# Mish in a fused attention, expert and MLP kernel: a square on ScalarE, the low half on VectorE

## The chip, the core and the metric

One core of one Trainium2 chip runs the whole program. Times are device microseconds (us) of one execution. TensorE (PE) does the matmuls, VectorE (DVE), ScalarE (ACT) and GpSimd (POOL) the elementwise work; each engine runs its own instructions strictly in the order in which the program issued them, and engines meet only at semaphores.

## What is computed

Causal attention over 4 batches of 8 heads and 576 positions, then a mixture of 8 experts with a capacity of 288 tokens each, and then, for every token, a second MLP with one set of weights. The part that the change touches is the activation of the second MLP:

```python
def _moe2_ref(x, w_in, w_out):          # x: 2304 x 512, w_in: 512 x 2048, w_out: 2048 x 512
    h = x @ w_in
    sp = np.where(h > 20.0, h, np.log1p(np.exp(np.minimum(h, 20.0))))
    g = h * np.tanh(sp)
    return (g @ w_out).astype(np.float32)
```

With a = e^h, tanh(log(1 + a)) is (a² + 2a) / (a² + 2a + 2), so that g can be had from Exp and Ln alone. `w_in` and `w_out` arrive as 64-bit floats.

## The kernel before, in words

Attention runs first, up to about 330 us; the routing of expert 0 follows. Then eight experts run one after the other, from 391 us on, and each has two stages. The up stage, `up(e)`, is the expert's own two matrices with Relu between them. The down stage, `down(e)`, takes the expert's 288 tokens through the second MLP. Both the experts and the second MLP work with split operands: every float32 matrix is a high half (rounded by ACT) and a low half (the rest), and each product is three matmuls, high by high, high by low, low by high (`mm3`, L444 to L446).

A down stage has 16 steps f, one for each 128 of the 2048 hidden rows. A step makes one PSUM tile `hp` by 12 matmuls (4 chunks by 3), hands it to `mish(f, p, gs)`, and then multiplies the finished activation of step f − 3 (`LAG = 3`) into four output tiles `y`, 12 matmuls again. In the first three steps there is no activation yet and only the first half is done; the last three have only the second half. `ps_h` has three `hp` banks.

The order on the engines is written out by hand. `tick()` is called in the middle and at the end of each half step, so there are four ticks in a full step. A tick runs what `later(n, ...)` had put n ticks ahead, then one step of `conv`, then perhaps one step of the routing of the next expert, `route(e + 1)`, whose VectorE operations (masks L248, one-hot blocks `ohs` L355, and many small ones) and small matmuls (`rt`, L253 to L360) so stand between those of the second MLP.

`mish` as it was: L531 takes min(h, 20) out of PSUM (DVE), L532 is Exp (ACT). Two ticks later `part1`: L535 b = (a + 2)·a on DVE, L536 Ln(b + 2) and L537 Exp(−) on ACT, L538 t = b·h on DVE, which is the last reader of the `hp` bank. Four ticks after the start `part2`: L542 t·a on DVE, L543 the high half by ACT (a Copy that rounds), L544 the low half by POOL. In the last two steps the delays are one and two ticks. `a`, `b` and `t` are three tiles of a ring `c1` of six.

Other work on the same engines: `split` of the expert weights (L413 ACT, L414 POOL), and in the first down stage still the conversion of the second MLP's weights from 64-bit words. A unit of that takes three DVE operations, L101, L104 and L107, on a tile of the same ring `c1`, one operation a tick, and then L83 on ACT and L84 on POOL.

Of the kernel before, what the change touches and what calls it, by code (L numbers as in the profile page):

```python
# [8 lines left out]
F32 = mybir.dt.float32  # L9
F32R = mybir.dt.float32r  # L10
# [4 lines left out]
AF = mybir.ActivationFunctionType  # L15
OP = mybir.AluOpType
# [7 lines left out]
CAP = N // E  # L24
# [3 lines left out]
def fb(ap):  # L28
    return ap.bitcast(F32)


class Convert:
    """The second MLP's weights: raw words to float32, split into hi and lo, in resident tiles."""

    def __init__(self, nc, w_in, w_out, ring):
        self.nc, self.w_in, self.w_out, self.ring = nc, w_in, w_out, ring
# [5 lines left out]
        self.steps = self.run()  # L42

    def slots(self):
        """Places for float32 words ahead of the split, in tiles that the experts need only later."""
        NC = DM // 128
        for name, n, words in (("xu", 1, 2 * NC * CAP), ("act", 4, 2 * CAP), ("ot", 1, NC * CAP)):
            for _ in range(n):
                t = self.ring(name, [128, words], I32)
                for j in range(words // 256):  # L50
                    yield t[:, 256 * j:256 * j + 256].rearrange("p (c f) -> p c f", c=2)
# [64 lines left out]


def constants(nc, one, K):
    """The expert choice's constants, one instruction or two a step."""

    def new(name, shape, dt):
        K[name] = one.tile(shape, dt, name=name)
        return K[name]

    def iota(name, shape, dt, pattern, base, mult):
        nc.gpsimd.iota(new(name, shape, dt), pattern=pattern, base=base, channel_multiplier=mult,
                       allow_small_or_imprecise_dtypes=True)

    iota("jj", [128, 63], F32, [[1, 63]], 1, 0)
    yield  # L130
    nc.gpsimd.memset(new("onesb", [128, 128], BF16), 1.0)
    yield
    upper = new("upper", [128, 128], BF16)
    nc.gpsimd.memset(upper, 1.0)
    yield
    nc.gpsimd.affine_select(out=upper, in_=upper, pattern=[[1, 128]], compare_op=OP.is_gt, fill=0.0,
                            base=0, channel_multiplier=-1)
    yield
    iota("slots", [128, CAP // 3], FP16, [[1, CAP // 3]], 0, 0)
    yield  # L140
    aux = new("aux", [128, NT, 3, 2], BF16)[:, :, 0]
    nc.gpsimd.iota(aux[:, 0:16, 0].rearrange("p (b i) -> p b i", b=B), pattern=[[S, B], [128, 4]], base=0,
                   channel_multiplier=0, allow_small_or_imprecise_dtypes=True)
    yield
    for r in range(2):
        nc.gpsimd.iota(aux[64 * r:64 * r + 64, 16:18, 0], pattern=[[2 * S, 2]], base=512 + 512 * r,
                       channel_multiplier=0, allow_small_or_imprecise_dtypes=True)
        yield
    nc.gpsimd.iota(aux[:, :, 1], pattern=[[0, NT]], base=0, channel_multiplier=1,
                   allow_small_or_imprecise_dtypes=True)  # L150
    yield
    iota("erow", [128, E], F32, [[-1, E]], E, 0)
    yield
    jj, th1, j20 = K["jj"], new("th1", [128, 63], I32), new("j20", [128, 63], F32)
    x1 = j20.bitcast(I32)
    nc.vector.tensor_scalar(th1, jj, -32.0, float(2 ** 26), op0=OP.add, op1=OP.mult)
    yield
    nc.vector.tensor_scalar(x1, th1, 31, 0x7FFFFFFF, op0=OP.arith_shift_right, op1=OP.bitwise_and)
    yield
    nc.vector.tensor_tensor(th1, th1, x1, op=OP.bitwise_xor)  # L160
    yield
    nc.vector.tensor_scalar(j20, jj, float(2 ** 20), None, op0=OP.mult)
    yield
    K["steps"] = []
    at = 20
    for i, nb in enumerate((5, 5, 5, 5)):
        at -= nb
        r = new(f"jr{i}", [128, 2 ** nb - 1], F32)
        nc.vector.tensor_scalar(r, jj[:, :2 ** nb - 1], float(2 ** at), None, op0=OP.mult)
        K["steps"].append((2 ** nb - 1, float(2 ** at), r))  # L170
        yield
    nc.vector.memset(new("cb", [128, 2 * NT], F32)[:, 0:1], 4096.0)


def build(ctx, tc, q, k, v, s, w_gate, w1, w2, w_in, w_out, out, debug=None):
# [22 lines left out]
    with ExitStack() as actx:  # L198
        attention(actx, tc, const, cv, q, k, v, s, w_gate, ident, L, x_dram, b_dram, constants(nc, const, K))
# [9 lines left out]
def experts(ctx, tc, K, ring, ident, L, x_dram, w1, w2, cv, out):  # L209
    nc = tc.nc  # L210
    NF1, NF2, NC, NJ, JW = F // 128, F2 // 128, DM // 128, 3, CAP // 3
    rot = ctx.enter_context(tc.tile_pool(name="m_rot", bufs=2))
    one = ctx.enter_context(tc.tile_pool(name="m_one", bufs=1))
# [8 lines left out]
    WI, WO = cv.WI, cv.WO  # L222

    jj, onesb, upper, slots, aux, erow, th1, j20, cb = (K[n] for n in (
        "jj", "onesb", "upper", "slots", "aux", "erow", "th1", "j20", "cb"))
    steps = K["steps"]
# [163 lines left out]
    raw, wt = {}, {}  # L390
# [61 lines left out]
    def later(n, fn, *args):  # L452
        todo.setdefault(now[0] + n, []).append((fn, args))
# [71 lines left out]
    spacer = one.tile([1, 1], F32, name="spacer")  # L525

    def mish(f, p, gs):
        a = rot.tile([128, CAP], F32, name="c1", bufs=6)
        b = rot.tile([128, CAP], F32, name="c1", bufs=6)
        t = rot.tile([128, CAP], F32, name="c1", bufs=6)  # L530
        nc.vector.tensor_scalar(a, p[:, :CAP], 20.0, None, op0=OP.min)  # L531
        nc.scalar.activation(a, a, AF.Exp)  # L532

        def part1():
            nc.vector.scalar_tensor_tensor(b, a, 2.0, a, op0=OP.add, op1=OP.mult)  # L535
            nc.scalar.activation(a, b, AF.Ln, bias=2.0)  # L536
            nc.scalar.activation(a, a, AF.Exp, scale=-1.0)  # L537
            nc.vector.tensor_mul(t, b, p[:, :CAP])  # L538

        def part2():  # L540
            g = ring("act", [128, 2, CAP], F32R)
            nc.vector.tensor_mul(t, t, a)  # L542
            nc.scalar.activation(g[:, 0], t, AF.Copy)  # L543
            nc.gpsimd.tensor_sub(g[:, 1], t, fb(g)[:, 0])  # L544
            gs[f] = g
        tail = f >= NF2 - 2
        later(1 if tail else 2, part1)
        later(2 if tail else 4, part2)

    def down(e):  # L550
        x2 = X2.pop(e)
# [3 lines left out]
        for f in range(NF2 + LAG):  # L555
            if f < NF2:
                need(f, 0)
                p = ps_h.tile([128, 512], F32, name="hp")
                for c in range(NC):
                    mm3(p[:, :CAP], (WI[f][:, 0, c], WI[f][:, 1, c]), (x2[:, 0, c], x2[:, 1, c]),  # L560
                        c == 0, c == NC - 1)
                    if c == 1:
                        tick()
                mish(f, p, gs)
                if f > 1:
                    feed(0 if f < NF2 - 6 else 1)
                tick()
            if f == NF2 and e + 1 < E:
                while side["route"] is not None:
                    tick()  # L570
                feed()
            if f >= NF2 and e + 1 < E:
                make_xt(e + 1, [f - NF2])
            if f >= LAG:
                need(f - LAG, 1)
                g = gs.pop(f - LAG)
                w = WO[f - LAG]
                for c in range(NC):
                    cs = slice(128 * c, 128 * c + 128)
                    mm3(o[c][:, :CAP], (w[:, 0, cs], w[:, 1, cs]), hl(g), f == LAG, f == NF2 + LAG - 1)  # L580
                    if c == 1:
                        tick()
                tick()
# [540 lines left out]
```

## Time and profile before

| | us |
|---|---|
| median of 3 runs | 1151.33 (1151.16 to 1170.0) |
| span of the profiled execution | 1157.2 |
| busy in that span: PE, DVE, ACT, POOL | 1018.5, 820.7, 569.4, 556.7 |

The profile is of one execution, and its span runs from the first to the last instruction; here it is 5.9 us over the median of the runs shown, so that a sum made in the span is carried to the median as a difference. The profile lists, for each engine and line, how long its instructions took and what ended the idle time before them, and it can be cut to a stretch of the span. An instruction's time is from its start to its end; where it had to wait for something after it had started, that is in its time and not in the idle time.

### The profile page before, as it was taken

The numbers are of one execution on the slowest core, as the hardware profiler recorded it, in microseconds if no ns is written. First come the engines' busy times: TensorE is split into PE (matmuls) and PEld (weight loads), VectorE is DVE, ScalarE is ACT, GpSimd is POOL, SyncE is SP. The second block draws the span as 40 slices with busy tenths as digits, with TensorE's granted clock in tenths as the row PEclk, the third lists the DMA queues.
The fourth block names the chain that finished last, engine by engine and source line by source line (L and its number), as shares of the span: only waits on it lengthen the run. The fifth ranks groups of instructions, "written<-read, shape, count | busy, mean of one in ns | idle before, by whom it ended". The sixth has DMA issues, their size and how long they took to land. (4 is left out here: it accounts for less than half of the span.)

```text
span 1157.2 us, 21785 instructions
## 1 busy us (share of the span) xinstructions
PE 1018.5 (88%) x7739; PEld 955.5 (83%) x7739; DVE 820.7 (71%) x2137; ACT 569.4 (49%) x1269; POOL 556.7 (48%) x567
## 2 busy tenths in 40 slices
PE   6889899889941778799999999999999999999996
PEld 5778788778830778788998988998899898899996
DVE  7566577777579889976876876776677577687274
ACT  5466557555751335443553553454454355355453
POOL 6355556455556653554256256256235324625622
PEclk8798889887875789999999999999999899999998
DMA  5687898887132532322123123023012112312300
GB/s 113 135 167 157 183 185 181 172 183 174 50 94 93 166 117 64 120 62 71 38 58 94 38 58 94 1 87 96 6 56 86 48 38 62 90 38 57 95 1 21
DMA packets 133657, 105.60 MB, mean 91 GB/s; under 512 B 63052, under 2 KB 113388, under 8 KB 133516
## 3 DMA queue, kind: packets, MB, share of 16 engines
q1 hardware_dynamic: 121596, 83.49, 30.2%
q10 hardware_dynamic: 8880, 11.27, 3.1%
q0 software_dynamic: 3072, 9.44, 2.7%
q8 instruction: 61, 1.00, 0.4%
q14 instruction: 48, 0.39, 0.1%
HBM read 69.55 MB, written 9.73 MB: 69 GB/s over the span
## 5 line engine op out<-in xcount | busy, mean ns | idle before, releaser
L544 POOL TENSOR_TENSOR act<-c,act 128x288 fp32r<-128x288 f32 x128 | 105.6, 826 | 295.8 <-ACT act L543 283.4
L945 POOL TENSOR_TENSOR Pl<-P,Ph 128x384 fp32r<-128x384 f32 (+2 forms) x128 | 136.1, 1068 | 135.1 <-DVE Ph L944 47.4
L414 POOL TENSOR_TENSOR wt<-raw,wt 128x512 fp32r<-128x512 f32 x128 | 169.0, 1335 | 64.5 <-ACT wt L413 62.6
L444 PE MATMUL y<-act,WO 128*128 128x288 f32 x512 | 157.3, 307 | 0.4
L445 PE MATMUL y<-act,WO 128*128 128x288 f32 x512 | 153.1, 299 | 3.7 <-POOL act L544 3.2
L444 PE MATMUL hp<-xu,WI 128*128 128x288 f32 x512 | 154.7, 302 | 0.0
L446 PE MATMUL y<-act,WO 128*128 128x288 f32 x512 | 152.1, 297 | 0.0
L445 PE MATMUL hp<-xu,WI 128*128 128x288 f32 x512 | 152.1, 297 | 0.0
L446 PE MATMUL hp<-xu,WI 128*128 128x288 f32 x512 | 151.6, 296 | 0.0
L535 DVE SCALAR_TENSOR_TENSOR c<-c 128x288 f32<-128x288 f32 x128 | 88.8, 694 | 49.7 <-ACT c L532 49.7
L543 ACT ACTIVATE act<-c 128x288 fp32r<-128x288 f32 x128 | 56.9, 445 | 112.5 <-DVE c L542 107.6
L413 ACT ACTIVATE wt<-raw 128x512 fp32r<-128x512 f32 x128 | 79.6, 624 | 56.0 <-PE y L446 29.1
L445 PEld LDWEIGHTS y<-act,WO 128*128 128x128 f32 x512 | 97.3, 190 | 6.2 <-POOL act L544 5.5
L444 PEld LDWEIGHTS y<-act,WO 128*128 128x128 f32 x512 | 97.3, 190 | 5.8 <-ACT c L532 2.1
L446 PEld LDWEIGHTS y<-act,WO 128*128 128x128 f32 x512 | 97.5, 190 | 0.0
L444 PEld LDWEIGHTS hp<-xu,WI 128*128 128x128 f32 x512 | 97.2, 190 | 0.3
L445 PEld LDWEIGHTS hp<-xu,WI 128*128 128x128 f32 x512 | 97.2, 190 | 0.0
L446 PEld LDWEIGHTS hp<-xu,WI 128*128 128x128 f32 x512 | 97.1, 190 | 0.0
L937 ACT ACTIVATE P<-s 128x384 f32<-128x384 f32 (+2 forms) x128 | 64.1, 503 | 62.5 <-PE s L930 42.7
L536 ACT ACTIVATE c<-c 128x288 f32<-128x288 f32 x128 | 57.0, 445 | 74.5 <-DVE c L535 74.4
L499 DVE SCALAR_TENSOR_TENSOR act<-hp,act 128x288 fp32r<-128x288 f32 x64 | 29.1, 454 | 86.2 <-ACT act L498 86.2
L966 PE MATMUL pv<-Ph,VH 128*128 128x320 f32 (+4 forms) x224 | 79.2, 354 | 5.2 <-DVE xT L985 5.1
(219 smaller groups left out, 3003.7 us busy)
## 6 DMA issues: line engine op xcount, KB each, us to landing
raw<-in_moe_w_dram SPq DMA_DIRECT2D x128, 256.0 KB
QKB<-qk SPq DMA_DIRECT2D x26, 576.0 KB
QKA<-qk SPq DMA_DIRECT2D x14, 576.0 KB
r<-in_moe_w_out_dram ACTq DMA_DIRECT2D x22, 256.0 KB
r<-in_moe_w_in_dram ACTq DMA_DIRECT2D x21, 256.0 KB
qkraw<-in_q_dram SPq DMA_DIRECT2D x32, 128.0 KB
qkraw<-in_k_dram SPq DMA_DIRECT2D x32, 128.0 KB
vraw<-in_v_dram SPq DMA_DIRECT2D x32, 128.0 KB
```

The source lines that it names most:

```text
L413: nc.scalar.activation(t[:, 0], r, AF.Copy)
L414: nc.gpsimd.tensor_sub(t[:, 1], r, fb(t)[:, 0])
L444: nc.tensor.matmul(out_ap, ah, bh, start=first, stop=False)
L445: nc.tensor.matmul(out_ap, ah, bl, start=False, stop=False)
L446: nc.tensor.matmul(out_ap, al, bh, start=False, stop=last)
L535: nc.vector.scalar_tensor_tensor(b, a, 2.0, a, op0=OP.add, op1=OP.mult)
L536: nc.scalar.activation(a, b, AF.Ln, bias=2.0)
L543: nc.scalar.activation(g[:, 0], t, AF.Copy)
L544: nc.gpsimd.tensor_sub(g[:, 1], t, fb(g)[:, 0])
L937: nc.scalar.activation(P[:, :n], p[:, :n], AF.Exp, scale=0.125)
L945: nc.gpsimd.tensor_sub(Pl[:, :n], P[:, :n], fb(Ph)[:, :n])
L966: nc.tensor.matmul(o, VH[i][:m, a, hs], ph, start=first, stop=False)
```

## The change

The activation is written as h − 2h/((e^h + 1)² + 1). ACT does Exp, then Square(a + 1), Ln(a + 1) and Exp(−), one right after the other and all on the tile `a` in place. Four ticks later (two in the last two steps) `product` makes (a − 0.5)·h on DVE, straight from PSUM, and ACT writes the high half as −2 times that. One tick later `low` makes the low half on DVE. `b`, `t`, `part1` and `part2` are gone, and POOL has no part in it any more. (In three other places comment strings are dropped.)

```diff
     def mish(f, p, gs):
+
         a = rot.tile([128, CAP], F32, name="c1", bufs=6)
-        b = rot.tile([128, CAP], F32, name="c1", bufs=6)
-        t = rot.tile([128, CAP], F32, name="c1", bufs=6)
         nc.vector.tensor_scalar(a, p[:, :CAP], 20.0, None, op0=OP.min)
         nc.scalar.activation(a, a, AF.Exp)
-
-        def part1():
-            nc.vector.scalar_tensor_tensor(b, a, 2.0, a, op0=OP.add, op1=OP.mult)
-            nc.scalar.activation(a, b, AF.Ln, bias=2.0)
-            nc.scalar.activation(a, a, AF.Exp, scale=-1.0)
-            nc.vector.tensor_mul(t, b, p[:, :CAP])
-
-        def part2():
+        nc.scalar.activation(a, a, AF.Square, bias=1.0)
+        nc.scalar.activation(a, a, AF.Ln, bias=1.0)
+        nc.scalar.activation(a, a, AF.Exp, scale=-1.0)
+
+        def product():
+            nc.vector.scalar_tensor_tensor(a, a, 0.5, p[:, :CAP], op0=OP.subtract, op1=OP.mult)
             g = ring("act", [128, 2, CAP], F32R)
-            nc.vector.tensor_mul(t, t, a)
-            nc.scalar.activation(g[:, 0], t, AF.Copy)
-            nc.gpsimd.tensor_sub(g[:, 1], t, fb(g)[:, 0])
+            nc.scalar.activation(g[:, 0], a, AF.Copy, scale=-2.0)
+            later(1, low, g)
+
+        def low(g):
+            nc.vector.scalar_tensor_tensor(g[:, 1], a, -2.0, fb(g)[:, 0], op0=OP.mult, op1=OP.subtract)
             gs[f] = g
-        tail = f >= NF2 - 2
-        later(1 if tail else 2, part1)
-        later(2 if tail else 4, part2)
+        later(2 if f >= NF2 - 2 else 4, product)
```

## Rows read from the trace of the kernel before

**Rows 1.** Busy time by stretch: first down stage, its middle, a later down stage.
```profile
core 0: us, PE busy (x) PEld busy (x) DVE busy (x) ACT busy (x) POOL busy (x), PEclk, DMA share, GB/s
434.70:509.70 75.00, 61.45 (x457) 59.02 (x457) 67.26 (x168) 37.98 (x90) 36.90 (x40) 0.93 0.28 86
...
545.20:603.70 58.50, 56.86 (x457) 54.49 (x457) 46.15 (x120) 31.02 (x73) 21.55 (x23) 1.00 0.17 47
...
446.00:503.00 57.00, 45.51 (x340) 43.53 (x339) 52.61 (x131) 27.92 (x66) 30.95 (x34) 0.95 0.34 101
```

**Rows 2.** Waits of TensorE in the first down stage: total us, times, longest.
```profile
PE rt L360 <- DVE ohs L355: 5.3, 3, 3.3
PE rt L262 <- DVE f1b L260: 3.2, 2, 2.1
```

**Rows 3.** Waits of TensorE from 510 us to the end.
```profile
PE rt L253 <- DVE mask L248: 14.5, 12, 2.4
PE rt L360 <- DVE ohs L355: 4.4, 18, 0.5
PE y L445 <- POOL act L544: 2.8, 6, 0.5
...
PE y L445 <- POOL spacer L605: 0.5, 1, 0.5
```

**Rows 4.** Lines of VectorE, 446 to 503 us: count, busy, mean ns, idle before.
```profile
L107 DVE SCALAR_TENSOR_TENSOR c<-r,c 128x256 int32<-128x256 int32 x14 | 8.6, 612 | 0.1
L535 DVE SCALAR_TENSOR_TENSOR c<-c 128x288 f32<-128x288 f32 x12 | 8.2, 685 | 2.1 <-ACT c L532 2.1
L542 DVE TENSOR_TENSOR c<-c,c 128x288 f32<-128x288 f32 x13 | 7.7, 595 | 0.5 <-ACT c L537 0.5
L104 DVE SCALAR_TENSOR_TENSOR c<-r,c 128x256 int32<-128x256 int32 x14 | 7.0, 497 | 0.1
L538 DVE TENSOR_TENSOR c<-c,hp 128x288 f32<-128x288 f32 x12 | 5.5, 454 | 0.8
L531 DVE TENSOR_SCALAR c<-hp 128x288 f32<-128x288 f32 x12 | 5.3, 446 | 0.0
```

**Rows 5.** The activation's line of GpSimd, 446 to 503 us.
```profile
L544 POOL TENSOR_TENSOR act<-c,act 128x288 fp32r<-128x288 f32 x13 | 12.0, 922 | 14.7 <-ACT act L543 14.7
```

**Rows 6.** Order of time on ScalarE in the last down stage: start, us, line.
```profile
1128.42 0.43 ACT L532 ACTIVATE c<-c 128x288 f32<-128x288 f32 x1
1129.76 0.45 ACT L536 ACTIVATE c<-c 128x288 f32<-128x288 f32 x1 [0.91 <-DVE c L535]
1130.23 0.45 ACT L537 ACTIVATE c<-c 128x288 f32<-128x288 f32 x1
1131.28 0.45 ACT L543 ACTIVATE act<-c 128x288 fp32r<-128x288 f32 x1 [0.61 <-DVE c L542]
1131.63 0.43 ACT L532 ACTIVATE c<-c 128x288 f32<-128x288 f32 x1
```

**Rows 7.** The same stretch on VectorE.
```profile
1130.71 0.46 DVE L542 TENSOR_TENSOR c<-c,c 128x288 f32<-128x288 f32 x1 [0.43 <-ACT c L537]
1131.09 0.45 DVE L531 TENSOR_SCALAR c<-hp 128x288 f32<-128x288 f32 x1
1132.09 0.85 DVE L535 SCALAR_TENSOR_TENSOR c<-c 128x288 f32<-128x288 f32 x1 [0.56 <-ACT c L532]
```

**Rows 8.** The same stretch on GpSimd.
```profile
1131.81 0.82 POOL L544 TENSOR_TENSOR act<-c,act 128x288 fp32r<-128x288 f32 x1 [2.40 <-ACT act L543]
```

**Rows 9.** Order of time on TensorE: one group of three matmuls, and the next.
```profile
1127.80 0.29 PE L444 MATMUL y<-act,WO 128*128 128x288 f32 x1
...
1128.19 0.30 PE L444 MATMUL y<-act,WO 128*128 128x288 f32 x1
```

**Rows 10.** A conversion step on VectorE with GpSimd idle.
```profile
439.96 0.42 DVE L107 SCALAR_TENSOR_TENSOR c<-r,c 128x256 int32<-128x256 int32 x1
```

**Rows 11.** ScalarE's only table load in the whole span.
```profile
0.83 1.28 ACT L181 ACT_TABLE_LOAD   x1 [0.83 <-PEq L1106]
```

## The prediction

> **What bounds the kernel now.** I first cut the span into stages by stretch. A later down stage takes 58.5 us and TensorE is busy for 56.86 of them at the full granted clock (2.4 GHz, 1.00); the other down stages that route an expert look the same. Such a stage is TensorE's, and an elementwise engine can give back there only what TensorE waits. The first down stage does the same matmuls in 75.0 us, with TensorE busy for 61.45 and VectorE for 67.26; in its middle VectorE has 52.61 of 57.00 us (92%), TensorE 45.51 [rows 1]. There VectorE sets the pace, because the weight conversion (L101 to L107) stands in its queue as well. The list of TensorE's waits, read next, says the same: in the first down stage it waits for blocks and flags that VectorE makes too late [rows 2]. From 510 us to the end its waits are 14.5 us for masks, which fall in the up stages, where no activation runs, 4.4 for `ohs`, and 2.8 and 0.5 at the end of the down stages, for the last low half [rows 3]. (The 0.5 names L605, the instruction on GpSimd after that low half.)
>
> So there are two places to look: VectorE's load in one stage, and the length of the chain from `hp` to the low half in all eight.
>
> **VectorE's load.** Per tile the change takes away L535, L542 and L538 and adds `product` and `low`; L531 stays. In the middle of the first down stage the three cost 8.2 + 7.7 + 5.5 = 21.4 us [rows 4]. `product` reads one operand from PSUM and one from SBUF, as L538 does: 12 × 0.454 = 5.5 us. `low` reads two operands from SBUF. The nearest rows are L542 with GpSimd idle, 0.46 us [rows 7], and L535 in this stretch, 0.685 [rows 4]: 5.5 to 8.2 us. L544 is gone but GpSimd keeps 30.95 − 12.0 = 19 us of work there [rows 1, 5], so I take 6.5. Saved: 21.4 − 12.0 = 9.4 us.
>
> The second part is contention. L535 started at 1132.09 took 0.85 us while L544 ran from 1131.81 to 1132.63 [rows 7, 8]; L542, of the same size, takes 0.46 when GpSimd is idle [rows 7]. The operation lasted until GpSimd had finished, and about 0.3 us longer. The conversion's steps show the same: L107 takes 0.42 with GpSimd idle [rows 10] and 0.612 on average here, L104, of the same shape, 0.497 [rows 4]. That is 14 × 0.19 + 14 × 0.08 = 3.8 us of waiting, and L544 is 12.0 of GpSimd's 30.95: I take 1.5, bounds 0 and 3.8. The Trainium skill (SBUF — State Buffer, "Who interferes with whom") states it as a rule: a DVE instruction with two SBUF inputs and a GpSimd instruction that reads SBUF exclude each other. By the rule `low` stays exposed to the weight splits on GpSimd, and would at worst take L535's 0.685, which is the upper bound already used.
>
> VectorE's load so falls by 10.9 us (7 to 14), from 52.6 to about 41.7 in 57. At the share of 92% that would be 45.3 us, below TensorE's own 45.51 [rows 1]: TensorE becomes the bound. With some of its waits left (route steps still sit among conversion steps) I put the stretch at 47, so 10 us gained. As a check, the floor of the whole stage is the later stage's 58.5 us, plus the loss of clock: the granted clock is 0.93 [rows 1], of which half-speed periods cost some 0.07 × 75 = 5 us. 75 − 10 = 65 lies just above 63.5. **First down stage: −10 us**, bounds −16.5 (all the way to 58.5) and −3.
>
> **ScalarE and the loop between the engines.** ScalarE gains an operation of about 0.45 us per tile: four become five, 5 × 0.45 = 2.25 us for each step of TensorE, which is 24 matmuls of (1128.19 − 1127.80)/3 = 0.13, so 3.12 us [rows 6, 9]. Even with the conversion's and split's copies it isn't full (37.98 of 75 us in the first down stage, 31.02 of 58.5 later [rows 1]; 16 × 0.45 = 7.2 more).
>
> On ScalarE the squaring costs 0.45 us, by the row of Ln or Exp [rows 6]; on VectorE the operation that it replaces, L535, costs 0.46 (as L542 with GpSimd idle) to 0.85 [rows 7]. The Trainium skill (ScalarE: Activation LUTs, "Rules for kernel authors") speaks against this edit: additions and multiplications belong on VectorE. By the rule the edit would bring a tile nothing or a loss; by the rows it is even at worst, and here VectorE is the fuller engine.
>
> More important than load is the order. ScalarE, in order, does Exp, Square, Ln, Exp of tile f, then the Copy of f, then Exp of f + 1; VectorE does `product` of f, then L531 of f + 1. That closes a loop from Exp to the next Exp. Before, it goes through both engines twice: 1128.42 to 1131.63, 3.21 us [rows 6], a trace more than TensorE's 3.12, so that the activation falls slowly behind. After: three dependent starts at 0.47 (1129.76 to 1130.23), the last Exp 0.45, 0.03 to VectorE, `product` 0.46, 0.11 back, and 0.35 from the Copy's start to the next Exp's [rows 6, 7] = 2.81 us. L531 of f + 1, which starts 0.38 after `product` [rows 7], is ready at the same moment. `low` stands behind L531 and waits for the Copy, but the next `product` comes only 1.9 us after the next Exp, so it is out of the loop, even when it waits for a weight split. The low half is there earlier: about 0.5 + 2.81 + 0.5 = 3.8 us after `hp`, against 0.5 + 3.21 + 0.9 with GpSimd at the end.
>
> What the `hp` bank sees is the opposite: it was free after L538 and is free now after `product`, some 0.4 us later. The next use of a bank starts 2.5 steps, 7.8 us, after its tile is complete, and `product` ends about 2.85 us after that: covered by 5 us. The ring `c1` loses two of three tiles per step, a relief only.
>
> **The other down stages.** The last low half: 2.8 + 0.5 us of waiting [rows 3] go, since it comes earlier and the loop no longer drifts: −3.3. Of the 4.4 us for `ohs` I take half, −2.2, as VectorE gets to them sooner. Against it, the start of a down stage: its first three steps have only 12 matmuls, 1.56 us. Two chains on ScalarE stand ahead of the first Copy: 0.5 (L531) + 2 × (3 × 0.47 + 0.35) + 0.45 + 0.11 + 0.46 = 5.0 us until the first low half is ready, and TensorE wants it at 3 × 1.56 + 0.13 = 4.8: up to 0.25 us late, eight times: +2, or 0 where a route step delays TensorE. Sum **−3.5 us**; bounds −7.7 (every wait gone, no late start) and +2 (none gone). GpSimd's relief itself, 105 us over the span, is worth nothing beyond this: in the later down stages it is busy for 21.55 of 58.5 us [rows 1].
>
> **Sum:** −10 − 3.5 = −13.5. The profiled execution's span of 1157.2 would be 1143.7; the median of the runs shown, 5.9 below that span, goes from 1151.33 to 1138.
>
> **Rivals.** (1) *More: all of VectorE's lateness goes.* The first down stage becomes a later one (−16.5, the clock too) and every wait listed for the others goes (−7.7): −24, to 1127. For it: VectorE ends below TensorE's need. Against: conversion steps still share each tick with the route. 13%. (2) *Hidden anyway.* In the first down stage the loop with one conversion step per round in it (2.81 + 0.42, and a route step) and the half-clock periods hold the pace, −3, and the others give nothing: 1148. For it: the row of L535 shows 2.1 us of idle time for ScalarE even there [rows 4]. 17%. (3) *Slower: the loop outgrows TensorE's step.* Place: ScalarE's queue, where the Copy of f bars Exp of f + 1. VectorE's other work in a later down stage is 46.15 − 16 × 2.1 = 12.6 us [rows 1, 4], 0.8 per step; if all of it fell between `product` and L531, the loop would be 3.6 us. It decides once 16 × (loop − 3.12) exceeds the 5 us of cover of the `hp` bank, from 3.43 us on; at 3.6 a stage loses 16 × 0.48 − 5 = 2.7 us, eight times 21, less the 10 of the first: 1162. Against: only one tick in four puts its work there. 7%. (4) *Square isn't in the loaded table.* One load of 1.28 us serves the whole span [rows 11], Exp, Ln, Copy and Relu all. If Square had to be switched to and back, ScalarE would need 2.25 + 2.56 = 4.8 us a step, 1.7 over TensorE's: 128 × 1.7 = +217, to 1355. For it: Square is new here; against: the loaded table already serves four functions, two of them simple. 2%.
>
> **How the numbers follow.** The forecast, a gain of 6 to 20 us, holds 61%; it gives 1138. With rivals (1) and (2) the range is 1123 to 1150, which leaves out (3), (4) and the far side of (1). A change of 2%, 23 us, is about what a measurement of this kernel can tell from none: faster by more needs rival (1) in full, 0.10; slower by more needs +23, rival (4) or a worse (3), 0.04; within, 0.86.
>
> **What would show it.** The first down stage at about 65 us with VectorE's share clearly below 92%; waits for `ohs` and flags there mostly gone; L107 nearer 0.5 than 0.6. In the last down stage a loop of about 2.8 us, then waits of L531 for `hp` (TensorE leads), and no wait of the last low half. Wrong would be: a first down stage that stays over 70 us, TensorE waiting at the first low half by more than 0.5 us, or `hp` banks waited for.

## The result and the profile after

The changed kernel takes 1124.97 us (median of 4, 1124.37 to 1131.49) against 1152.24 for the kernel before: a ratio of 0.975, 95% interval 0.971 to 0.980, so about 27 us faster. Measured a second time, the same kernel gave 1134.4 against 1152.8, a ratio of 0.983 (0.977 to 0.990), 18 us; the stages below, which repeat better, changed by 24. 1138 had been forecast, a gain of 13.5: the direction was right, and the size was about half.

Stages of the changed kernel, as in [rows 1]: the first down stage, its middle, and a later down stage.

```profile
core 0: us, PE busy (x) PEld busy (x) DVE busy (x) ACT busy (x) POOL busy (x), PEclk, DMA share, GB/s
...
425.30:493.30 68.00, 58.43 (x457) 55.99 (x457) 57.64 (x152) 44.55 (x106) 21.57 (x24) 0.97 0.32 95
436.00:493.00 57.00, 49.00 (x378) 47.22 (x377) 48.74 (x127) 36.92 (x88) 19.58 (x22) 0.97 0.35 103
529.00:584.90 55.90, 55.57 (x457) 54.39 (x457) 34.39 (x104) 39.02 (x89) 7.99 (x7) 1.00 0.17 49
```

The first down stage falls from 75.0 to 68.0 us, a later one from 58.5 to 55.9. VectorE has 9.6 us less to do in the first and 11.8 less in a later one, where GpSimd falls from 21.55 to 7.99 and ScalarE rises by 8.

What TensorE waits for from the end of the first down stage on (answers [rows 3]; total us, times, longest):

```profile
PE rt L253 <- DVE mask L248: 13.4, 11, 2.5
PE hp L475 <- DMA xg<-x_dram,idx: 0.8, 4, 0.3
PE hp L475 <- issue: 0.8, 1, 0.8
```

From this list the waits for `ohs` and for the last low half are gone; the masks, which belong to the up stages, are nearly as they were. In the first down stage some stay, and one for an `hp` bank is new (answers [rows 2]; L537 is `product`, the bank's last reader):

```profile
PE rt L360 <- DVE ohs L355: 3.4, 2, 2.3
...
PE rt L262 <- DVE f1b L260: 1.8, 2, 1.2
...
PE hp L444 <- DVE c L537: 0.4, 1, 0.4
```

And the loop in the last down stage, on ScalarE and VectorE (answers [rows 6, 7]; in the new file L530 is the minimum, L531 to L534 the four steps on ScalarE, L537 `product`, L539 the high half, L543 `low`):

```profile
1094.18 0.44 ACT L531 ACTIVATE c<-c 128x288 f32<-128x288 f32 x1 [0.27 <-DVE c L530]
...
1095.61 0.45 ACT L534 ACTIVATE c<-c 128x288 f32<-128x288 f32 x1
1096.63 0.45 ACT L539 ACTIVATE act<-c 128x288 fp32r<-128x288 f32 x1 [0.58 <-DVE c L537]
1097.35 0.45 ACT L531 ACTIVATE c<-c 128x288 f32<-128x288 f32 x1 [0.27 <-DVE c L530]
```
```profile
1093.69 0.46 DVE L530 TENSOR_SCALAR c<-hp 128x288 f32<-128x288 f32 x1 [0.31 <-PE hp L446]
1094.06 0.45 DVE L543 SCALAR_TENSOR_TENSOR act<-c,act 128x288 fp32r<-128x288 f32 x1
1096.09 0.46 DVE L537 SCALAR_TENSOR_TENSOR c<-c,hp 128x288 f32<-128x288 f32 x1 [1.57 <-ACT c L534]
```

VectorE now waits 0.31 us for each `hp` in this stretch: TensorE leads, the period of 3.17 us is TensorE's, and the loop has slack.

Summed by stage over the two profiles that each kernel has (the second ones are the runs `e1_before_again` and `e7_after_again` below), the part from the first up stage on goes from 766.3 and 761.8 to 742.6 and 737.8 us, a mean of −23.8: the first down stage −7.5, the six later ones that route −2.55 each, −15.3, the last −0.6, the up stages −0.4. What the first pair of spans shows beyond that, 11 us before the first up stage, is not the change's (first experiment).

### The profile page after: what moved, and what is told of

It reads as the page before. It is cut to its first block, busy times and chain, and to the rows that moved or that the text cites. A ratio compares the mean times of both kernels' runs of the same rounds, so it can differ in the third digit from the quotient of the medians.

```text
span 1122.6 us, 21462 instructions
## 1 busy us (share of the span) xinstructions
PE 989.3 (88%) x7739; PEld 933.8 (83%) x7739; DVE 726.6 (65%) x2009; ACT 631.5 (56%) x1397; POOL 447.7 (40%) x439
## 4 chain that ended last, share of the span: by engine, by line
PE 37%; DVE 21%; issue 17%; DMA 10%; ACT 8%; SPq 3%; POOL 3%; ACTq 0%; POOLq 0%; DVEq 0%
PE y L444 5%; PE y L446 4%; PE y L445 4%; PE hp L444 4%; PE hp L445 4%; PE hp L446 4%; DMA QKA<-qk 3%; POOL wt L414 3%; DVE mask L248 2%; DMA xg<-x_dram,idx 2%; PE rt L253 2%; SPq L651 2%; DVE cx L280 2%; DVE c L107 1%; DVE c L104 1%
## 5 line engine op out<-in xcount | busy, mean ns | idle before, releaser
L414 POOL TENSOR_TENSOR wt<-raw,wt 128x512 fp32r<-128x512 f32 x128 | 165.2, 1305 | 378.6 <-ACT wt L413 364.8
L537 DVE SCALAR_TENSOR_TENSOR c<-c,hp 128x288 f32<-128x288 f32 x128 | 57.7, 451 | 86.8 <-ACT c L534 85.4
L413 ACT ACTIVATE wt<-raw 128x512 fp32r<-128x512 f32 x128 | 79.7, 624 | 57.4 <-PE y L446 23.6
L539 ACT ACTIVATE act<-c 128x288 fp32r<-128x288 f32 x128 | 56.5, 442 | 54.3 <-DVE c L537 50.6
L531 ACT ACTIVATE c<-c 128x288 f32<-128x288 f32 x128 | 56.5, 441 | 53.6 <-DVE c L530 49.7
L530 DVE TENSOR_SCALAR c<-hp 128x288 f32<-128x288 f32 x128 | 58.1, 454 | 42.7 <-PE hp L446 40.8
L543 DVE SCALAR_TENSOR_TENSOR act<-c,act 128x288 fp32r<-128x288 f32 x128 | 68.0, 532 | 21.3 <-ACT act L539 18.5
```

The lines of the kernel that those rows point to most:

```text
L413: nc.scalar.activation(t[:, 0], r, AF.Copy)
L414: nc.gpsimd.tensor_sub(t[:, 1], r, fb(t)[:, 0])
L537: nc.vector.scalar_tensor_tensor(a, a, 0.5, p[:, :CAP], op0=OP.subtract, op1=OP.mult)
L539: nc.scalar.activation(g[:, 0], a, AF.Copy, scale=-2.0)
L543: nc.vector.scalar_tensor_tensor(g[:, 1], a, -2.0, fb(g)[:, 0], op0=OP.mult, op1=OP.subtract)
```

## The experiments

Three theories on the gain. G: GpSimd's subtraction held VectorE's operations, which is contention. W: VectorE had fewer operations to do. L: the loop through ScalarE became shorter than TensorE's step. A fourth, P, came up on the way: the low half itself came late, as GpSimd made it. The table has the stages of each kernel's profile; "later" is the mean of the six later down stages that route; single ones lie up to 1.1 us from it, most within 0.4.

| kernel | first down stage, us | later, us | median us | ratio to before (95%) |
|---|---|---|---|---|
| before, two profiles | 75.0, 74.7 | 58.4, 58.4 | | |
| after, two profiles | 68.0, 66.5 | 55.9, 55.9 | | |
| e2_before_low_on_dve | 74.0 | 56.3 | 1138.3 | 0.992 (0.987 to 0.997) |
| e3_after_dummy_gpsimd | 70.9 | 55.9 | 1136.6 | 0.989 (0.980 to 0.999) |
| e4_after_more_dve | 74.6 | 56.2 | 1141.8 | 0.995 (0.991 to 1.000) |
| e5_after_longer_chain | 72.9 | 57.4 | 1155.1 | 1.000 (0.996 to 1.004) |
| e6_after_low_on_gpsimd | 67.5 | 56.8 | 1136.9 | 0.986 (0.979 to 0.994) |
| e8_first_low_on_gpsimd | 67.6 | 55.9 | 1132.5 | 0.981 (0.971 to 0.990) |

The medians of one kernel differ by up to 1% between chips and runs, so stages decide here, not totals. The first down stage is the least sure of them: the changed kernel's two profiles differ by 1.5 us there, those of the kernel before by 0.3.

Below, "by starts" means: the time from each matmul's start to the next one's, summed by what the next one is (a block's, a flag's, one that needs an activation's halves, one for gathered rows), per later down stage, against the mean of the changed kernel's two profiles.

**The kernel before, again.** No edit.

> The kernel before, unchanged, profiled a second time. In the first pair of profiles 11 us of the 34.6 us between the two spans lie before 391 us, where both programs run the same instructions. If that part is chance of the clock, this profile has the first up stage beginning somewhere between 380 and 391 us, the later down stages (those that route an expert) again at 57.7 to 58.8 us and the first down stage at 73 to 77 us, and the ratio is 1.00. If the part is a real effect of the change, it begins at 391 us again, within 2 us.

Ratio 1.003 (0.998 to 1.008). The stages repeat within 0.3 us, but the first up stage begins at 386.0 us, not 391.0. In all the profiles here, with the same instructions ahead of that point, it begins between 380.0 and 396.3 us. So the 11 us in the first pair of profiles are not the change's, and the changed kernel's first profile was the luckiest; what sets this part's length isn't shown.

**One part alone: the low half on VectorE.**

```diff
...
             nc.scalar.activation(g[:, 0], t, AF.Copy)
-            nc.gpsimd.tensor_sub(g[:, 1], t, fb(g)[:, 0])
+            later(1, low, g)
+
+        def low(g):
+            nc.vector.tensor_sub(g[:, 1], t, fb(g)[:, 0])
             gs[f] = g
```

> The arithmetic of before, but its low half on VectorE, one tick after the high half: one part of the change alone. Theory G (GpSimd's subtraction held VectorE's two-operand instructions, and that made the small route steps late): nearly all of the gain of the later down stages is here, 58.5 to about 56.3 us, and the first down stage goes from 75 to about 71. Theory W (the number of VectorE's operations): VectorE now has five a tile instead of four, so the first down stage gets no better than 75 and the later ones stay at 58 or more. Theory L (the loop through ScalarE, 3.21 us before): the loop falls to about 2.85 here, because L535 falls from 0.85 to 0.46, so L too expects about 56.3 in the later stages.

The later stages take 2.1 of the 2.5 us with them; the first gains less than 1. So W falls for the later stages (VectorE has an operation more, and they are faster) and fits the first. G, L and P all fit the later stages. G and L are not even rivals here. On ScalarE in the last down stage of this kernel:

```profile
1113.82 0.45 ACT L532 ACTIVATE c<-c 128x288 f32<-128x288 f32 x1 [0.24 <-DVE c L531]
1114.79 0.45 ACT L536 ACTIVATE c<-c 128x288 f32<-128x288 f32 x1 [0.53 <-DVE c L535]
```

From Exp to Ln it is 0.97 us, against 1.34 in the kernel before [rows 6], where L535 stood beside GpSimd's low half [rows 7, 8] and lasted 0.85 us. With that gone the loop has 0.24 us to wait for the next minimum and keeps TensorE's 3.17. So it was contention that made the old loop, at 3.21, too long: these engines also hold each other where no semaphore is between them. By starts the time ahead of `ohs` is as in the changed kernel but for one stage of the six, and 0.6 us is left around the activations' halves.

**Contention put back.**

```diff
...
             nc.scalar.activation(g[:, 0], a, AF.Copy, scale=-2.0)
+            nc.gpsimd.tensor_sub(junk, a, fb(g)[:, 0])
             later(1, low, g)
```

> The changed kernel with GpSimd's old subtraction put back beside it, same operands, same place, result thrown away: contention without a dependence and without a longer loop (product reads PSUM and one SBUF operand). Theory G: the later down stages return from 55.8 to 57 or more, the first from 68 to 71 or more, total +10 to +16 us. Theories W and L: nothing moves, later stages 55.8 to 56.0, first 68 to 69, total within 3 us of the changed kernel.

Contention alone costs the later stages nothing once the loop has slack: 55.9 us, not a tenth more, although the operations are held. That doesn't clear it in the kernel before, whose loop had none. Lines of VectorE in a later stage of this kernel (a later numbering: L538 is `product`) against the changed one:

```profile
L538 DVE SCALAR_TENSOR_TENSOR c<-c,hp 128x288 f32<-128x288 f32 x16 | 7.2, 452 | 7.0 <-ACT c L535 6.9
L355 DVE TENSOR_TENSOR ohs<-slots,sr 128x576 bf16<-128x576 f16 x3 | 4.1, 1363 | 0.0
```
```profile
L537 DVE SCALAR_TENSOR_TENSOR c<-c,hp 128x288 f32<-128x288 f32 x16 | 7.2, 451 | 10.4 <-ACT c L534 10.4
L355 DVE TENSOR_TENSOR ohs<-slots,sr 128x576 bf16<-128x576 f16 x3 | 2.2, 749 | 0.0
```

`ohs` takes 1.36 us instead of 0.75, and TensorE doesn't notice, since VectorE has 10.4 us of waiting for the last Exp to spend in the stage, of which 7.0 are left. In the first stage, where it has 4.8 us of such time, the same dummy costs 3.6 us against the mean of the two profiles after.

**Load put back on VectorE.**

```diff
...
+        def more():
+            for _ in range(2):
+                nc.vector.tensor_scalar(junk, p[:, :CAP], 20.0, None, op0=OP.min)
+        later(1 if f >= NF2 - 2 else 2, more)
         later(2 if f >= NF2 - 2 else 4, product)
```

> The changed kernel with two more operations a tile on VectorE, two ticks after the start, each reading PSUM alone and writing a scratch tile: load (0.75 us a tile, as much as the change took away by count) without contention with GpSimd. Theory W: the first down stage returns from 68 to 73 or more and the later ones from 55.8 to 57 or more. Theories G and L: the later stages stay within 0.4 us of 55.8; in the first, where VectorE is 85% busy, up to +4 us.

First stage 74.6, the whole gain given back; later stages +0.3. VectorE is busy for 68.5 us in the first stage, 10.8 more than in the changed kernel, where the change had taken 9.6. So W alone is enough to explain the first stage; e3 and e5 show that it isn't the only thing that costs there. The granted clock of that stage is 0.93 in this run and in the next, 0.97 in the changed kernel; how much of the time is the clock's isn't separated.

**The loop made longer than TensorE's step.**

```diff
...
         nc.scalar.activation(a, a, AF.Exp, scale=-1.0)
+        nc.scalar.activation(a, a, AF.Copy)
...
```

> The changed kernel with a fifth operation in ScalarE's chain, an in-place copy between the last Exp and product: the loop from one Exp to the next grows by 0.47 us, from 2.81 to 3.28 by the rows, so over TensorE's 3.15 as it was before (3.21); VectorE's and GpSimd's work is unchanged. Theory L (the length of the loop set the later down stages): they return from 55.9 to 57.5 us or more, with waits for the route's blocks and for the last low half. Theory P (the low half came late because GpSimd made it, in 0.82 us): they stay at 55.8 to 56.3. The first down stage, by both, 68 to 71.

Later stages 57.4 us, 1.5 us slower, and the whole kernel as slow as before. On ScalarE in the last down stage (L540 is the high half here), and what TensorE waits for in that stage:

```profile
1118.72 0.43 ACT L531 ACTIVATE c<-c 128x288 f32<-128x288 f32 x1
...
1121.64 0.45 ACT L540 ACTIVATE act<-c 128x288 fp32r<-128x288 f32 x1 [0.58 <-DVE c L538]
1122.00 0.43 ACT L531 ACTIVATE c<-c 128x288 f32<-128x288 f32 x1
```
```profile
PE y L444 <- ACT act L540: 3.0, 3, 2.1
PE hp L444 <- DVE c L538: 0.3, 1, 0.3
```

The period is 3.28 us, what the prediction's sum plus 0.47 gives, and over TensorE's 3.17: 66.3 us instead of 61.3. Falling back by 0.11 a step makes little more than 1 us of these 5; the start of the stage makes most of the rest. At the fifth `hp` the minimum starts 2.1 us after its tile's last matmul ends (1.1 in the changed kernel). The loop with slack wins that back, to 0.04 by the eighth; this one is 3.1 behind at the 15th, and TensorE pays at the end.

Theory L expected waits for the route's blocks and for the last low half in the later stages, and these did not come: by starts the time ahead of `ohs` and around the halves is the changed kernel's within 0.1 us. The 1.5 us stand ahead of flags (+0.9) and of gathered rows (+0.5), where the change had gained nearly nothing. So a loop over TensorE's step costs, but this run doesn't show that 1.5 of the change's 2.5 us were the loop's: `ohs` stood inside the old loop and stands outside this one. The copy also gives ScalarE 6 us more work a stage (45.2 of 57.8 us busy). The first stage expected 68 to 71 and took 72.9, so there the chain counts as well as the load.

**The low half back on GpSimd.** The activation is carried with its sign turned, so that GpSimd can subtract, and the sign is turned back where the output leaves PSUM.

```diff
...
-        nc.scalar.activation(a, a, AF.Ln, bias=1.0)
+        nc.scalar.activation(a, a, AF.Ln, scale=0.5, bias=0.5)
...
-            nc.vector.scalar_tensor_tensor(a, a, 0.5, p[:, :CAP], op0=OP.subtract, op1=OP.mult)
+            nc.vector.scalar_tensor_tensor(a, a, 1.0, p[:, :CAP], op0=OP.subtract, op1=OP.mult)
...
-            nc.scalar.activation(g[:, 0], a, AF.Copy, scale=-2.0)
+            nc.scalar.activation(g[:, 0], a, AF.Copy)
...
-            nc.vector.scalar_tensor_tensor(g[:, 1], a, -2.0, fb(g)[:, 0], op0=OP.mult, op1=OP.subtract)
+            nc.gpsimd.tensor_sub(g[:, 1], a, fb(g)[:, 0])
...
```

> The changed kernel with the low half on GpSimd again (the activation is carried with its sign turned, and turned back where the output is copied out of PSUM, so that a plain subtraction does): the loop stays at 2.81 us, VectorE loses one operation a tile, GpSimd makes the low half in 0.82. Theory L: later down stages 55.7 to 56.3. Theory P: 57.5 or more. For the first down stage, theory W (VectorE's work, +6.6 us for two operations a tile more) expects about 65 us, theory G (contention with GpSimd, +2.9 us with the dummy) about 71; together 67 to 68.

56.8, between the two: in the new order, GpSimd's low half costs 0.9 us a stage. By starts 0.7 of it is around the halves, of 1.2 that the change had freed there. GpSimd's order of time shows how (L414 splits an expert's weight, L373 gathers its rows, L543 is the low half):

```profile
759.73 1.30 POOL L414 TENSOR_TENSOR wt<-raw,wt 128x512 fp32r<-128x512 f32 x1 [1.44 <-ACT wt L413]
760.97 0.82 POOL L543 TENSOR_TENSOR act<-c,act 128x288 fp32r<-128x288 f32 x1
761.93 0.95 POOL L373 DMA_INDIRECT xg<-x_dram,idx  x1
763.19 0.93 POOL L373 DMA_INDIRECT xg<-x_dram,idx  x1 [0.30 <-issue]
764.42 0.92 POOL L373 DMA_INDIRECT xg<-x_dram,idx  x1 [0.31 <-issue]
765.37 2.32 POOL L543 TENSOR_TENSOR act<-c,act 128x288 fp32r<-128x288 f32 x3
```

In the last steps each low half stands in GpSimd's queue behind a weight split of 1.29 us that waits for ScalarE first, and then three of them stand behind three gathers; they come at once. In the kernel before the queue was another: there the split stood behind the low half, and of the last three low halves one waited for the gathers and the others for ScalarE. GpSimd of that kernel in a later stage:

```profile
779.68 0.92 POOL L373 DMA_INDIRECT xg<-x_dram,idx  x1 [0.30 <-issue]
780.62 0.81 POOL L544 TENSOR_TENSOR act<-c,act 128x288 fp32r<-128x288 f32 x1
782.39 0.81 POOL L544 TENSOR_TENSOR act<-c,act 128x288 fp32r<-128x288 f32 x1 [0.96 <-ACT act L543]
785.60 0.81 POOL L544 TENSOR_TENSOR act<-c,act 128x288 fp32r<-128x288 f32 x1 [2.40 <-ACT act L543]
```

So the 0.9 us can't be carried over as P's share of the change; a low half that comes late because ScalarE was late is the loop's. In the first stage, 67.5, VectorE loses 16 operations of 0.60 us, and its busy time falls by only 1.4: the conversion's L107 takes 0.70 us instead of 0.56. TensorE also waits 2.6 us there for GpSimd's low half. What the operation saves, contention and lateness give back.

**The changed kernel, again.** No edit.

> The changed kernel, unchanged, profiled a second time. The stages repeat: first down stage 67 to 69 us, later ones 55.7 to 56.4, last 61.3. The start of the first up stage, 380 us in the first profile and 386 to 396 in the runs since, all with the same instructions ahead of it, is somewhere between 380 and 396; the ratio to the kernel before lies at 0.975 to 0.99.

Ratio 0.983 (0.977 to 0.990), median 1134.4. First stage 66.5, a little under the expectation, later stages 55.6 to 56.7, start of the first up stage at 385.4.

**A mixture: GpSimd in the first stage only.**

```diff
...
-            nc.vector.scalar_tensor_tensor(g[:, 1], a, -2.0, fb(g)[:, 0], op0=OP.mult, op1=OP.subtract)
+            (nc.gpsimd if e == 0 else nc.vector).tensor_sub(g[:, 1], a, fb(g)[:, 0])
...
```

> The low half on GpSimd in the first down stage alone, where VectorE is the fullest engine, and on VectorE in the other seven (with the sign turned, as in the run before). Theories W and G together: first down stage 65 to 68 us, so 0 to 3 better than the changed kernel; later stages as there, 55.7 to 56.4. If contention outweighs the operation saved, 69 to 71.

67.6 and 55.9: the changed kernel's stages. It doesn't beat it; in the first stage TensorE waits 2.6 us for the low half, as with the low half on GpSimd throughout.

## Why the prediction was right in direction and wrong in size and place

**The first down stage: −10 forecast, −7.5 measured.** The step held in direction. VectorE's load set that stage, but it fell by less than was taken: by 9.6 us over 16 tiles, 0.60 a tile, where 10.9 over the 12 tiles of the middle had been forecast, 0.91 a tile. One term that was too large is contention, 1.5 us. In the middle of the changed kernel's stage:

```profile
L543 DVE SCALAR_TENSOR_TENSOR act<-c,act 128x288 fp32r<-128x288 f32 x15 | 9.1, 605 | 1.8 <-ACT act L539 1.8
L107 DVE SCALAR_TENSOR_TENSOR c<-r,c 128x256 int32<-128x256 int32 x14 | 8.2, 587 | 0.2
L104 DVE SCALAR_TENSOR_TENSOR c<-r,c 128x256 int32<-128x256 int32 x14 | 6.9, 490 | 0.2
```

L107 came to 0.587 us from 0.612, not nearer 0.5, and L104 hardly moved [rows 4]: 0.4 us in all. `low` took 0.605 where 0.54 was reckoned. The rows of VectorE overlap besides (L531 starts 0.38 us after a row of 0.46 [rows 7]), so that sums of rows overstate what leaves the queue. That TensorE "becomes the bound" held only in part: VectorE still has 86% of the middle (48.74 of 57.00), TensorE's waits for `ohs` and flags fell only from 5.3 and 3.2 us to 3.4 and 1.8, and a wait of 0.4 us for an `hp` bank came in. Load (e4), contention (e3) and chain (e5) each cost microseconds there, so no single one of them bounds it.

**The other down stages: −3.5 forecast, −15.9 measured. This is the step that failed**; two thirds of the gain came from stages that were to give a quarter. By starts (defined above), over the six later stages and the last, mean of two profiles of each kernel, its terms measured:

| term | forecast, us | measured, us |
|---|---|---|
| `ohs` | −2.2 | −8.0 |
| the halves of the last activations | −3.3 | −8.3 |
| late start of a stage | +2 | +1.1 |
| gathered rows | 0 | −0.7 |
| sum | −3.5 | −15.9 |

It was mis-sized in three ways.

First, "an elementwise engine can give back there only what TensorE waits", with the wait read from busy shares and from the list of idle times. Busy for 56.86 of 58.5 us [rows 1] leaves 1.64, and the stage fell by 2.55. The list counts a matmul's time until its modelled end. A matmul's row lasts 0.29 us while the next starts 0.13 after it [rows 9], so a wait shows only what exceeds the difference of 0.16, and shorter ones not at all. In order of time, before one block of the route in a later stage of the kernel before, and of the changed kernel:

```profile
769.89 0.29 PE L446 MATMUL y<-act,WO 128*128 128x288 f32 x1
770.39 0.43 PE L360 MATMUL rt<-aux,ohs 128*96 128x6 bf16 x6 [0.20 <-DVE ohs L355]
```
```profile
749.52 0.29 PE L446 MATMUL y<-act,WO 128*128 128x288 f32 x1
749.65 0.39 PE L360 MATMUL rt<-aux,ohs 128*96 128x6 bf16 x6
```

The list says 0.20 us; from start to start it is 0.50 against 0.13, a loss of 0.37. The Trainium skill (Perfetto Trace Analysis, "Identifying the Most-Contended Engine") says that matmul busy time is no good measure of how near a kernel is to its limit, because pipelined instructions look smaller in the trace; this trace agrees, with 1.64 us of a stage not busy and 2.55 to be had. The Trainium skill (Perfetto Trace Analysis, "Optimization Strategy") tells the reader to find the gaps between slices. In this trace a gap of TensorE is itself too small, by 0.16 us a wait.

Second, of the 4.4 us for `ohs` only half was taken. The prediction's own loop would have said more: in the steps with a block of the route, `ohs` stood between L538 and L542, so inside the old loop. On VectorE of the kernel before, in the same stage, and then of the changed kernel:

```profile
766.72 0.44 DVE L531 TENSOR_SCALAR c<-hp 128x288 f32<-128x288 f32 x1
767.72 0.83 DVE L535 SCALAR_TENSOR_TENSOR c<-c 128x288 f32<-128x288 f32 x1 [0.56 <-ACT c L532]
768.66 0.46 DVE L538 TENSOR_TENSOR c<-c,hp 128x288 f32<-128x288 f32 x1
769.03 1.30 DVE L355 TENSOR_TENSOR ohs<-slots,sr 128x576 bf16<-128x576 f16 x1
770.26 0.44 DVE L542 TENSOR_TENSOR c<-c,c 128x288 f32<-128x288 f32 x1
770.62 0.44 DVE L531 TENSOR_SCALAR c<-hp 128x288 f32<-128x288 f32 x1
```
```profile
744.77 0.46 DVE L530 TENSOR_SCALAR c<-hp 128x288 f32<-128x288 f32 x1 [0.65 <-PE hp L446]
745.14 0.69 DVE L543 SCALAR_TENSOR_TENSOR act<-c,act 128x288 fp32r<-128x288 f32 x1
745.76 0.74 DVE L355 TENSOR_TENSOR ohs<-slots,sr 128x576 bf16<-128x576 f16 x1
747.17 0.45 DVE L537 SCALAR_TENSOR_TENSOR c<-c,hp 128x288 f32<-128x288 f32 x1 [0.67 <-ACT c L534]
748.27 0.46 DVE L530 TENSOR_SCALAR c<-hp 128x288 f32<-128x288 f32 x1 [0.64 <-PE hp L446]
```

The period is 3.90 us there, not 3.21, and TensorE's own step, with the block's matmuls in it, is 3.50, as the changed kernel shows where VectorE waits for it. The difference of 0.40, three times a stage, is the 1.2 us lost ahead of the blocks. Both L535 (0.83) and `ohs` (1.30, beside a weight split on GpSimd) are held there. After the change `ohs` falls into the time in which VectorE waits for the last Exp. The price of the loop in the prediction was taken from the last down stage, the one without a route.

Third, GpSimd's relief was put at nothing, from its busy share of 21.55 in 58.5 us. Taking the low half off GpSimd, and nothing else, gave 2.1 of the 2.5 us of a later stage (e2). A share of busy time says nothing on whom an instruction holds or makes wait.

**What held:** the loop's sum, 2.81 us, is confirmed by e5 (2.81 + 0.47 = 3.28 measured). The late start of a down stage showed by starts, at about half its price: 0.4 us at the first low half of the last stage, and 0.1 ahead of a flag in each later one, where VectorE waits for the first high half. **The rivals:** (1), at 1127 with 13%, came nearest in time in the first measurement, though its mechanism was half right: the listed waits for `ohs` and the low half went, the first stage didn't reach 58.5. That the second measurement came to 1134, not far from 1138, is no merit of the sum: the stages of its profiled run show the same gain. (2) fell: the others gave more than the first stage. (3) is real but from the other side: it decides in e5, not in this change. No table load was added: (4) fell.

**What stays open:** moving the low half explains most of the later stages' gain (e2), the smaller load on VectorE that of the first (e4). How the 2.5 us of a later stage divide between contention, loop and late low halves isn't shown: no single change back (e3, e5, e6) brings back the 1.3 us of `ohs`. By the rows it took held operations inside a loop without slack; contention and the long chain together weren't run. How much of the first stage is load, chain or contention when all act at once can't be read from the single changes either.

## What to carry to other kernels

Where two in-order engines hand a tile back and forth, add up the loop from one tile's first step to the next one's, with everything that the program puts between them in the stages where it does, and compare it with the step of the engine that should lead: this loop was 0.04 us too long in a plain step, and 0.4 in a step with a block of the route in it. Slack in it is what wins a late start back. Size TensorE's waits from start to start, not from the gaps between its rows. And before an engine's relief is put at nothing for its low share, look at what its instruction holds and who waits for it.

## What the runs showed that was not expected

Contention between GpSimd and VectorE is cheap or dear by the stage alone: the same dummy subtraction, once a tile, made `ohs` 0.61 us longer in a later stage and cost it nothing, and cost about 3.6 us in the first. The part ahead of the experts, the same instructions in every kernel here, took from 380.0 to 396.3 us; between single profiles of whole programs, 16 us are no evidence.
